# Delta-rule attention with a rational MoE: a chunk's front six slots later, weights in 16 larger groups

## The chip, the cores and the metric

The kernel runs on one core of one Trainium2 chip. Its time is the time of one execution of the whole program in microseconds; the figure for a kernel is the median over several executions, and lower is better.

## What is computed

Two layers in a row. The first is a delta rule over 768 time steps for 4 batches x 8 heads with a head size of 48; the second a feed-forward layer with a rational activation on 3072 tokens (384 -> 2048 -> 384).

```python
k_n = k / (np.linalg.norm(k, axis=-1, keepdims=True) + 1e-06)
for t in range(S):
    kt, vt, bt = (k_n[:, :, t], v[:, :, t], beta[:, :, t, None])
    y[:, :, t] = np.einsum('bhd,bhde->bhe', q[:, :, t], state)
    v_old = np.einsum('bhde,bhd->bhe', state, kt)
    state = state + bt[:, :, :, None] * np.einsum('bhd,bhe->bhde', kt, vt - v_old)
...
x = np.ascontiguousarray(attn_out.transpose(0, 2, 1, 3)).reshape(B * S, H * D)
...
h = x @ w_in
h2 = h * h
h3 = h2 * h
P = a[0] + a[1] * h + a[2] * h2 + a[3] * h3
Q = 1.0 + np.abs(b[0]) * np.abs(h) + np.abs(b[1]) * h2
g = P / (Q + 1e-06)
return (g @ w_out).astype(np.float32)
```

The inputs of the layer's weights arrive as 64-bit floating-point numbers and are read as pairs of 32-bit words.

## The kernel before

**Chunks and units.** The 768 steps are cut into 12 chunks of 64. A chunk's attention gives 256 tokens, and the feed-forward layer of those tokens is cut into 8 units of 256 hidden columns each, so there are 96 units, n = 8c to 8c + 7 for chunk c. Every product is made of three half-precision passes on high and low parts.

**A unit** has `hidden` (18 products into the tile `ph`), `numerator` (two ScalarE operations, then L830, L832, L833 on VectorE), `quotient` (two ScalarE operations, then L844, L845, L846 on VectorE and one product on GpSimd) and `accumulate` (12 products into `po`). The unit's VectorE operations are kept in the order in which they are written. They work on the tiles `mr`, `mu`, `mw`, three buffers of each.

**A chunk's attention** is a row of steps. `ahead` loads k, v and q and normalises the keys. `front` has `keys_transposed` (a transposing DMA, then `kbd`), `key_products` (`pg`, copied to `g`, written to DRAM as `gd`), `inverse` (reads `gd` back as `gb`, some 30 small VectorE operations, the result `wh` goes to an image `img` in DRAM and comes back as `wc`), `scales`, `queries_transposed` and `query_products` (`pm`). `middle` has `off_blocks` (`pe` from `wc`, read out as `et`; `wc` also goes to the block-diagonal tile `wbd`), `state_split` and `residual`. `back` is the solve: `pu` from `wbd`, three steps in which `pu` is read out as `z` by ScalarE and VectorE and multiplied again, then the state (`pd`), the output (`py`), and `tokens`, which transposes the output (`px`) into `xT`, the right-hand side of `hidden`, and `scalars`, a row of one-column operations that ends in `msc` (L787). Both `hidden` and `numerator` of unit 8c need them.

**The order of the work.** Each of these steps is written in one of 8 slots (j) of a chunk. In the slots of unit group c the program writes the solve of chunk c + 1, the middle of c + 2, the front of c + 3 and the loads of c + 4:

```python
def attention(c, j):
    for f, cc in ((back, c + 1), (middle, c + 2), (front, c + 3), (ahead, c + 4)):
        if cc < NCH:
            f(cc, j)
```

The framework then sets the order on each engine at build time, by the order written, by priorities (the solve has a raised one) and by a model of times; on the chip each engine runs its list strictly in that order. DMAs are issued by SyncE (SP), which also keeps its order. The pools `ps_f` and `ps_c` of PSUM hold one tile each; `ps_f` serves `pg`, `pm`, `pe`, the sums of `scales` and, from chunk 3 on, `px`. A tile is handed on in the order written.

**The weights** are made first, among the attention of chunks 0 and 1: `load_in(i)` makes a unit's 768 columns in three groups of 256, `load_out(i)` in four of 192, 56 groups in all. `to_f32` turns a group of word pairs into 32-bit numbers: an absolute value on ScalarE, a minimum and maximum on GpSimd, a shift (L318) and two combining operations (L325) on VectorE. In `load_out` the second half is then split on GpSimd. The groups of `load_out` use as their lower limit the value `gate`, which the first inverse writes, and so come behind it.

Of the kernel before, what the change touches and what calls it, by code (L numbers as in the profile page):

```python
# [36 lines left out]
def kernel(  # L37
# [271 lines left out]
    def to_f32(t, src, nm, keep=MIN_NORMAL):  # L309

        n = t.shape[-1]
        st = staged([P, n, 2], U32, "ws" + nm)
# [5 lines left out]
        nc.vector.tensor_scalar(  # L318
            t, a.bitcast(U32), 3, KEEP, op0=ALU.logical_shift_left, op1=ALU.bitwise_and
        )  # L320
        for word, scalar, in1, op0, op1 in (
            (wh, 0xC0000000, t, ALU.bitwise_and, ALU.bitwise_or),
            (wl, 29, t, ALU.logical_shift_right, ALU.bitwise_or),
        ):
            nc.vector.scalar_tensor_tensor(out=t, in0=word, scalar=scalar, in1=in1, op0=op0, op1=op1)  # L325
# [3 lines left out]
    def load_in(i):  # L329
        w64 = moe_w_in.bitcast(U32)  # L330
        t = w_out[:, i].rearrange("p a b e -> p (a b e)").bitcast(U32).rearrange("p (c f) -> p c f", c=NCC)
# [13 lines left out]
        split16((w_in[:, i, 0], w_in[:, i, 1]), t.bitcast(F32), sw[:, 0, i : i + 1])  # L345

    def load_out(i):
        w64 = moe_w_out.bitcast(U32)
        if i + 1 < NU:
            to = w_out[:, i + 1].rearrange("p a b e -> p a (b e)").bitcast(U32)  # L350
            to = [to[:, j] for j in range(2)]
        else:
            to = [staged([P, DM], U32, f"wo32_{i}_{j}") for j in range(2)]
        fs = sb.tile([P, 2], F32, tag="wfs", name=f"wfs_{i}")
        for j in range(2):
            f = 2 * i + j
            for e in range(2):
                cl = slice(e * DM // 2, (e + 1) * DM // 2)
                to_f32(to[j][:, cl], w64[f * P : (f + 1) * P, e * DM : (e + 1) * DM], f"o{f}_{e}", gate)
            sum_squares(fs[:, j : j + 1], to[j].bitcast(F32), w_out[:, i, 0, j])  # L360
# [679 lines left out]
```

## Time and profile before

| | us |
|---|---|
| median of 3 runs | 845.66 (845.34 to 847.08) |
| the profiled execution | 849.25 |
| its span, from the first to the last instruction | 845.5 |
| busy in the span: PE (matmul) | 627.7 (74%) |
| VectorE (DVE) | 740.2 (88%) |
| ScalarE (ACT) | 617.1 (73%) |
| GpSimd (POOL) | 338.1 (40%) |
| mean granted clock of TensorE | 0.944 |

The profile is one execution. A row of a group gives line, engine, operation, output<-input, its form and count, then busy us and the mean ns of one, then the engine's idle time just before it and what ended that; a row of one line's records gives the shortest, median and longest duration in ns and the first and last start in us. "DMA to landing" is the time from the issue to the end of the transfer. L826 to L846 are a unit's operations.

### The profile page before, as it was taken

To read this page: it belongs to the slowest core of one execution; us is meant where nothing else is said; L and a number is where in the kernel's file an instruction comes from. 1 tells how busy PE (TensorE), PEld (TensorE's weight loads), DVE (VectorE), ACT (ScalarE), POOL (GpSimd) and SP (SyncE) were. 2 spreads that over 40 slices of the span, in tenths; PEclk is the share of its full clock that TensorE was granted. 3 is DMA by queue.
4 is the path that set the end of the run, shared out by engine and by line. 5 is a ranking of instruction groups with operands and counts; after the bars stand their busy time and mean duration, and the time that the engine had idled before them with its cause. 6 is when DMAs were issued, how large, how long until landed. Compare 5 with 4: busy or idle time off the path is not lost.

```text
span 845.5 us, 23179 instructions
## 1 busy us (share of the span) xinstructions
PE 627.7 (74%) x9264; PEld 493.8 (58%) x9264; DVE 740.2 (88%) x1405; ACT 617.1 (73%) x1278; POOL 338.1 (40%) x322
## 2 busy tenths in 40 slices
PE   0330346778778777866978988789789789999995
PEld 0220344666566666755866866667567667786662
DVE  5999896688879778987998999989988799998996
ACT  4866658768667675866966968768668768788873
POOL 6545754334435333253433433432433332222232
PEclk9999996898989898989999999989899999999999
DMA  8998979769979879999599399696597674300000
GB/s 237 249 212 170 225 155 170 123 140 169 157 130 165 146 120 191 146 140 183 93 145 187 71 176 150 119 193 105 98 167 111 110 103 80 76 2 21 1 19 19
DMA packets 466507, 111.46 MB, mean 132 GB/s; under 512 B 431328, under 2 KB 463072, under 8 KB 466400
## 3 DMA queue, kind: packets, MB, share of 16 engines
q1 hardware_dynamic: 464224, 108.83, 71.3%
q8 instruction: 72, 1.18, 0.6%
q10 hardware_dynamic: 2176, 1.17, 0.5%
q14 instruction: 35, 0.29, 0.1%
HBM read 40.47 MB, written 26.23 MB: 79 GB/s over the span
## 4 chain that ended last, share of the span: by engine, by line
DVE 34%; PE 19%; DMA 17%; SPq 11%; ACT 10%; issue 7%; POOL 1%; ACTq 0%; DVEq 0%; POOLq 0%
PE ph L808 7%; PE po L862 5%; DVE ph L845 4%; DVE w_out L325 4%; DVE mg L844 3%; DVE mw L830 3%; DVE mu L833 3%; DVE mu L832 3%; SPq L119 3%; PE pu L401 2%; DMA tq<-xdq 2%; DMA gd<-g 2%; DMA tk<-xdk 2%; SPq L475 2%; DVE mu L846 2%
## 5 line engine op out<-in xcount | busy, mean ns | idle before, releaser
L862 PE MATMUL po<-w_out,mg 128*128 128x384 f16 x1152 | 226.5, 339 | 33.3 <-DVE mg L844 20.9
L847 POOL TENSOR_TENSOR mg<-mu,mr 128x512 f16<-128x512 f32 x96 | 124.8, 1300 | 258.1 <-DVE mu L846 203.8
L808 PE MATMUL ph<-xT,w_in 128*128 128x256 f16 x1728 | 216.3, 280 | 14.1 <-DVE mu L846 11.2
L808 PEld LDWEIGHTS <-w_in 128*128 128x128 f16 x1728 | 169.8, 101 | 51.1 <-DVE mu L846 14.4
L862 PEld LDWEIGHTS <-mg 128*128 128x128 f16 x1152 | 109.5, 101 | 103.4 <-DVE mg L844 27.7
L401 PEld LDWEIGHTS <-kbd 128*128 128x128 f16 x1680 | 66.7, 109 | 47.8 <-issue 43.3
L830 DVE SCALAR_TENSOR_TENSOR mw<-mr,msc,ph 128x512 f32<-128x512 f32 x96 | 71.1, 741 | 22.1 <-ACT mu L828 21.9
L831 ACT ACTIVATE mw<-mw 128x512 f32<-128x512 f32 x96 | 60.4, 629 | 39.7 <-DVE mw L830 39.2
L845 DVE SCALAR_TENSOR_TENSOR ph<-mw,msc,mg 128x512 f32<-128x512 f32 x96 | 81.4, 848 | 1.0
L844 DVE SCALAR_TENSOR_TENSOR mg<-mu,msc,mr 128x512 f16<-128x512 f32 x96 | 81.1, 844 | 0.0
L826 ACT ACTIVATE mr<-ph,msc 128x512 f32<-128x512 f32 x96 | 65.2, 679 | 18.7 <-PE ph L808 6.9
L828 ACT ACTIVATE mu<-ph,coef,msc 128x512 f32<-128x512 f32 x96 | 74.2, 773 | 0.0
L846 DVE SCALAR_TENSOR_TENSOR mu<-mu,msc,ph 128x512 f32<-128x512 f32 x96 | 71.1, 741 | 1.4
L833 DVE SCALAR_TENSOR_TENSOR mu<-mu,msc,ph 128x512 f32<-128x512 f32 x96 | 70.7, 736 | 1.0
L841 ACT ACTIVATE mr<-mw,msc 128x512 f32<-128x512 f32 x96 | 69.2, 721 | 1.7
L401 PE MATMUL pu<-z,ebd 128*128 128x48 f16 x1728 | 54.9, 185 | 18.1 <-DVE z L232 13.5
L401 PEld LDWEIGHTS <-ebd 128*128 128x128 f16 x1728 | 53.9, 98 | 21.7 <-issue 19.4
L832 DVE TENSOR_TENSOR mu<-ph,mu 128x512 f32<-128x512 f32 x96 | 65.5, 682 | 0.0
L842 ACT ACTIVATE mr<-mr 128x512 f32<-128x512 f32 x96 | 60.3, 628 | 1.3
L401 PEld LDWEIGHTS <-wbd 128*128 128x128 f16 x1152 | 37.7, 99 | 35.9 <-issue 34.8
L230 POOL TENSOR_TENSOR mm<-m,mm 128x1024 f16<-128x1024 f32 x12 | 29.2, 2436 | 73.6 <-ACT mm L226 64.5
L401 PE MATMUL pm<-tq,kbd 128*128 128x64 f16 x576 | 27.0, 220 | 20.1 <-DMA tq<-xdq 18.3
(195 smaller groups left out, 1195.0 us busy)
## 6 DMA issues: line engine op xcount, KB each, us to landing
wsi<-in_moe_w_in_dram SPq DMA_DIRECT2D x24, 256.0 KB, 5.0
xdk<-kn SPq DMA_DIRECT2D x24, 256.0 KB, 3.7
kbd<-tk SPq DMA_DIRECT2D x24, 256.0 KB, 5.5
gd<-g SPq DMA_DIRECT2D x24, 256.0 KB, 3.5
...
```

The source lines that it names most:

```text
L401: nc.tensor.matmul(dst[p][:, h], head(bd, lp, p * H + h), head(rt, rp, p * H + h), start=start and n == 0 and h == 0, stop=stop and n == l ...
L808: nc.tensor.matmul(ph[:, i], w_in[:, f2, wp, cc, i * P : (i + 1) * P], x[:, xp, cc], start=k == 0, stop=k == 3 * NCC - 1,)
L828: nc.scalar.activation(u, ph, AF.Identity, scale=A3, bias=a2)
L830: in_order(nc.vector.scalar_tensor_tensor(out=w, in0=z, scalar=B0, in1=ph, op0=ALU.add, op1=ALU.mult))
L832: in_order(nc.vector.tensor_mul(u, ph, u))
L833: in_order(nc.vector.scalar_tensor_tensor(out=u, in0=u, scalar=A1, in1=ph, op0=ALU.add, op1=ALU.mult))
L841: nc.scalar.activation(r, w, AF.Ln, bias=Q0)
L844: in_order(nc.vector.scalar_tensor_tensor(out=g[:, 0], in0=u, scalar=A0, in1=r, op0=ALU.add, op1=ALU.mult))
L845: in_order(nc.vector.scalar_tensor_tensor(out=t, in0=w, scalar=Q0, in1=g[:, 0], op0=ALU.add, op1=ALU.mult))
L846: in_order(nc.vector.scalar_tensor_tensor(out=u, in0=u, scalar=A0, in1=t, op0=ALU.add, op1=ALU.subtract))
L847: nc.gpsimd.tensor_mul(g[:, 1], u, r)
L862: nc.tensor.matmul(po[p], g[:, gp, i, p * P : (p + 1) * P], w_out[:, f2, wp, i], start=f2 == lo and i == 0 and k == 0, stop=f2 == hi - 1 a ...
```

## The change

Three things:

1. `front` and `ahead` run six slots later against `back` and `middle` (`LATE`), and the parts of them that would be written ahead of the first unit are left to the slots; `off_blocks` moves from slot 3 to slot 4.
2. A weight group has 768 columns: one for each `load_in`, one for each `load_out`, 16 in all. The absolute value goes straight to its place; the split of `load_out` is one operation on ScalarE and one on VectorE, and GpSimd's half is gone. The last two groups of `load_in` take `gate` as their limit too.
3. `mr`, `mu` and `mw` become one tile `mx` of three parts, three buffers of it, in which the word pairs are also staged.

```diff
+        return sb.tile(shape, dtype, tag="mx", name=nm, bufs=MB)
...
-        nc.sync.dma_start(out=st.rearrange("p f w -> p (f w)"), in_=src)
+        parts_ = src.shape[1]
+        nc.sync.dma_start(out=st.rearrange("p (a f) w -> p a (f w)", a=parts_), in_=src)
...
-        a = sb.tile([P, n], F32, tag="mg", name="wa" + nm, bufs=MB)
-        nc.scalar.activation(a, wh.bitcast(F32), AF.Abs)
-        nc.gpsimd.tensor_scalar(a, a, 3.0e38, keep, op0=ALU.min, op1=ALU.max)
...
+        nc.scalar.activation(t.bitcast(F32), wh.bitcast(F32), AF.Abs)
+        nc.gpsimd.tensor_scalar(t.bitcast(F32), t.bitcast(F32), 3.0e38, keep, op0=ALU.min, op1=ALU.max)
+        nc.vector.tensor_scalar(t, t, 3, KEEP, op0=ALU.logical_shift_left, op1=ALU.bitwise_and)
...
-        for cc in range(NCC):
-            to_f32(t[:, cc], w64[cc * P : (cc + 1) * P, i * 4 * P : (i + 1) * 4 * P], f"i{i}_{cc}")
+        to_f32(t, w64[:, i * 4 * P : (i + 1) * 4 * P].rearrange("(c p) x -> p c x", p=P), f"i{i}", gate if i >= NU - 2 else MIN_NORMAL)
...
+        to_f32(t, w64[2 * i * P : (2 * i + 2) * P].rearrange("(j p) x -> p j x", j=2), f"o{i}", gate)
...
-            else:
-                scaled(to[j].bitcast(F32), ss[:, 1:2])
-                split16((w_out[:, i, 0, j], w_out[:, i, 1, j]), to[j].bitcast(F32), eng=nc.gpsimd)
+        split16((w_out[:, i, 0], w_out[:, i, 1]), t, ss[:, 1:2])
...
-        r = z = sb.tile([P, 2, TG], F32, tag="mr", name=f"mr{n}", bufs=MB)
+        m = sb.tile([P, 3, 2, TG], F32, tag="mx", name=f"mx{n}", bufs=MB)
+        u, w, r = (m[:, i] for i in range(3))
...
-        elif j == 3:
+        elif j == 4:
             with tc.high_priority(300):
                 off_blocks(c)
...
+    LATE = 6
+
     def attention(c, j):
-        for f, cc in ((back, c + 1), (middle, c + 2), (front, c + 3), (ahead, c + 4)):
+        for f, cc, late in ((back, c + 1, 0), (middle, c + 2, 0), (front, c + 3, LATE), (ahead, c + 4, LATE)):
+            cc, jj = divmod(cc * NU + j - late, NU)
             if cc < NCH:
-                f(cc, j)
+                f(cc, jj)
...
-            if what == "f":
+            if what == "f" and f0 * NU + j < 3 * NU - LATE:
...
-            elif what == "a":
+            elif what == "a" and (f2 + 1) * NU + j < 4 * NU - LATE:
```

In the rows of the changed kernel below, its own line numbers stand: L811, L813, L814, L825, L826, L827 are L830, L832, L833, L844, L845, L846 of before, L809 is L826, L768 is L787, L313 and L315 are L318 and L325, L718 and L720 are L737 and L739, L568, L572, L420 are L587, L591, L439. Numbers behind a name tell one tile from the next of its name.

**VectorE before unit 40**, the first of chunk 5. Before the change, from L844 of unit 38 on (the operations L844 to L846 of unit n - 1 are written behind L830 to L833 of unit n; `z_2` is the third step of the solve of chunk 6):

```order
L844 SCALAR_TENSOR_TENSOR mg_7689<-mu_7575,msc_6424,mr_7573 128x512
L501 RECIPROCAL nrm_8157<-nrm_8157 128x16
L617 TENSOR_SCALAR sc_7909<-pfq_7907 128x2
L845 SCALAR_TENSOR_TENSOR ph_7659<-mw_7577,msc_6424,mg_7689 128x512
L232 SCALAR_TENSOR_TENSOR z_2_7976<-pu_7589,zmask,z_2_7976 128x768
L619 TENSOR_SCALAR sc_7909<-sc_7909,sc_6798 128x1
L846 SCALAR_TENSOR_TENSOR mu_7575<-mu_7575,msc_6424,ph_7659 128x512
L787 TENSOR_TENSOR msc_7535<-tab,sf_7446 128x48
L251 TENSOR_SCALAR sc_7909<-lgq_7912 128x2
L545 TENSOR_TENSOR ab_8088<-gb_7900,bblk 128x64
L830 SCALAR_TENSOR_TENSOR mw_7837<-mr_7833,msc_7535,ph_7814 128x512
```

And after it, where `xT` and `msc` belong to chunk 5, the three `z` to the solve of chunk 6:

```order
L232 SCALAR_TENSOR_TENSOR z_0_7129<-pu_7004,zmask,z_0_7129 128x768
L232 SCALAR_TENSOR_TENSOR xT_6804<-px_6808,sf_6806,xT_6804 128x768
L750 RECIPROCAL kp_0_6878<-kp_0_6878 128x2
L232 SCALAR_TENSOR_TENSOR z_1_7315<-pu_7004,zmask,z_1_7315 128x768
L757 TENSOR_SCALAR kp_0_6878<-kp_0_6878,top 128x1
L251 TENSOR_SCALAR kp_0_6878<-kp_0_6878 128x1
L761 RECIPROCAL kp_0_6878<-kp_0_6878 128x1
L768 TENSOR_TENSOR msc_6900<-tab,sf_6806 128x48
L598 TENSOR_SCALAR sc_7064<-pfq_7062 128x2
L600 TENSOR_SCALAR sc_7064<-sc_7064,sc_5969 128x1
L232 SCALAR_TENSOR_TENSOR z_2_7422<-pu_7004,zmask,z_2_7422 128x768
L811 SCALAR_TENSOR_TENSOR mx_7301<-mx_7301,msc_6900,ph_7282 128x512
```

The making of `xT` and all three solve steps, which stood among the operations of the units ahead, now stand behind L846 of unit 38 and ahead of the first operation of unit 40 (`et` of chunk 6 comes a few rows ahead of them, behind L844 of unit 38). The same rows stand before units 48, 56, 64 and 72; before units 32 and 80 `et` comes earlier. The last operation of the inverse (`wh`) of chunk 6 stands behind L830 of unit 36 and `et` of chunk 6 behind that of unit 39; before the change they stood behind those of units 26 and 31.

**ScalarE at the same place**, after the change, up to the first operation of unit 40 (`g` and `gl` are of chunk 7):

```order
L228 ACTIVATE z_1_7315<-pu_7004,zmask 128x768
L742 ACTIVATE kp_0_6878<-kp_0_6878,coef 128x1
L742 ACTIVATE kp_0_6878<-kp_0_6878 128x1
L497 ACTIVATE g_6952<-pg_6903 128x1024
L758 ACTIVATE kp_0_6878<-kp_0_6878 128x1
L226 CAST gl_6956<-g_6952 128x768
L759 ACTIVATE kp_0_6878<-kp_0_6878 128x1
L742 ACTIVATE kp_0_6878<-kp_0_6878 128x1
L742 ACTIVATE sf_6806<-kp_0_6878 128x1
L742 ACTIVATE sf_6806<-sf_6806,kp_0_6878 128x1
L228 ACTIVATE z_2_7422<-pu_7004,zmask 128x768
L809 ACTIVATE mx_7301<-ph_7282,msc_6900 128x512
```

The reading out of `pg` of the next front but one and of the second and third solve step stands ahead of the unit's first operation. On TensorE the two small products of `px` come ahead of the 48 of `pu<-rr`, the transposes behind these, and `pg` and most of the 36 products of units 40 and 41 between the second and the third multiplication of the solve.

**SyncE behind the inverse of chunk 6**, before the change:

```order
L587 DMA img_129<-wh_6163 128x16x16
L119 DMA q_6426<-in_q_dram 64x8x48 x3
L591 DMA wc_6167<-img_129 64x16x64 x2
L119 DMA q_6426<-in_q_dram 64x8x48
L433 DMA kbd_115<-tk_5953 64x16x128 x2
L119 DMA k_6531<-in_k_dram 64x8x48 x3
L116 DMA v_6283<-in_v_dram 64x16x48 x2
L119 DMA k_6531<-in_k_dram 64x8x48
L439 DMA wbd_123<-gl_5577 64x16x96 x2
L518 DMA gd_6634<-g_6684 64x16x64 x2
L528 DMA gb_6789<-gd_6634 128x16x16
L439 DMA wbd_123<-wc_6167 64x16x128 x2
```

And after it:

```order
L568 DMA img_129<-wh_6275 128x16x16
L116 DMA v_7473<-in_v_dram 64x16x48 x2
L572 DMA wc_6279<-img_129 64x16x64 x2
L420 DMA wbd_123<-wc_6279 64x16x128 x2
L587 DMA ebd_121<-et_6634 16x32x48
L587 DMA ebd_121<-et_6634 16x32x32
```

The issues that stood between `wc` and `wbd` (loads, `kbd`, the next front's `gd` and `gb`) are no longer there.

More of the change, by code (lines that the diff above doesn't have):

```diff
@@ L312, in to_f32 @@
         st = staged([P, n, 2], U32, "ws" + nm)
-        nc.sync.dma_start(out=st.rearrange("p f w -> p (f w)"), in_=src)
+        parts_ = src.shape[1]
+        nc.sync.dma_start(out=st.rearrange("p (a f) w -> p a (f w)", a=parts_), in_=src)
         wl, wh = st[..., 0], st[..., 1]
-        a = sb.tile([P, n], F32, tag="mg", name="wa" + nm, bufs=MB)
-        nc.scalar.activation(a, wh.bitcast(F32), AF.Abs)
-        nc.gpsimd.tensor_scalar(a, a, 3.0e38, keep, op0=ALU.min, op1=ALU.max)
[L318 to L325, printed above, removed]
+        nc.scalar.activation(t.bitcast(F32), wh.bitcast(F32), AF.Abs)
+        nc.gpsimd.tensor_scalar(t.bitcast(F32), t.bitcast(F32), 3.0e38, keep, op0=ALU.min, op1=ALU.max)
+        nc.vector.tensor_scalar(t, t, 3, KEEP, op0=ALU.logical_shift_left, op1=ALU.bitwise_and)
+        for word, scalar, op0 in ((wh, 0xC0000000, ALU.bitwise_and), (wl, 29, ALU.logical_shift_right)):
+            nc.vector.scalar_tensor_tensor(out=t, in0=word, scalar=scalar, in1=t, op0=op0, op1=ALU.bitwise_or)
     def load_in(i):
         w64 = moe_w_in.bitcast(U32)
-        t = w_out[:, i].rearrange("p a b e -> p (a b e)").bitcast(U32).rearrange("p (c f) -> p c f", c=NCC)
-        for cc in range(NCC):
-            to_f32(t[:, cc], w64[cc * P : (cc + 1) * P, i * 4 * P : (i + 1) * 4 * P], f"i{i}_{cc}")
+        t = w_out[:, i].rearrange("p a b e -> p (a b e)").bitcast(U32)
+        to_f32(t, w64[:, i * 4 * P : (i + 1) * 4 * P].rearrange("(c p) x -> p c x", p=P), f"i{i}", gate if i >= NU - 2 else MIN_NORMAL)
+        t = t.bitcast(F32).rearrange("p (c f) -> p c f", c=NCC)
         s2 = w_in[:, i, 0].bitcast(BF16)
-        nc.scalar.activation(s2, t.bitcast(F32), AF.Square)
+        nc.scalar.activation(s2, t, AF.Square)
         pf = ps_h.tile([P, 2 * P], F32, tag="h", name=f"pfw{i}")
@@ L344, in load_in @@
         scale_of(sw[:, 0, i : i + 1], ss, f"w{i}")
-        split16((w_in[:, i, 0], w_in[:, i, 1]), t.bitcast(F32), sw[:, 0, i : i + 1])
+        split16((w_in[:, i, 0], w_in[:, i, 1]), t, sw[:, 0, i : i + 1])
     def load_out(i):
@@ L349, in load_out @@
         if i + 1 < NU:
-            to = w_out[:, i + 1].rearrange("p a b e -> p a (b e)").bitcast(U32)
-            to = [to[:, j] for j in range(2)]
-        else:
[L353 to L360, printed above, removed]
+            t = w_out[:, i + 1].rearrange("p a b e -> p (a b e)").bitcast(U32)
+        else:
+            t = staged([P, 2 * DM], U32, f"wo32_{i}")
+        to_f32(t, w64[2 * i * P : (2 * i + 2) * P].rearrange("(j p) x -> p j x", j=2), f"o{i}", gate)
+        t = t.bitcast(F32).rearrange("p (j e) -> p j e", j=2)
+        fs = sb.tile([P, 1], F32, tag="wfs", name=f"wfs_{i}")
+        sum_squares(fs, t, w_out[:, i, 0])
         ss = sb.tile([P, 2], F32, tag="ss", name=f"vss_{i}")
-        nc.vector.tensor_scalar(ss[:, 0:1], fs[:, 0:1], fs[:, 1:2], 2.0 ** -30, op0=ALU.add, op1=ALU.max)
+        nc.vector.tensor_scalar_max(ss[:, 0:1], fs, 2.0 ** -30)
         ro = sw[:, 1, i : i + 1]
```

11 lines of the change are left out of this document (1 added, 10 removed).

## The prediction

> **What bounds the kernel now.** I read the page's span first, then the busy time by stage, cut where the records of L830 (a unit's first operation on VectorE) open units 0, 8, 16, 24, 80 and 88, and then the groups by line and the DMAs' times to landing for the steps that move. Columns of the stages: stretch and its length, then busy time of each engine, the clock, the DMA share and GB/s.
>
> ```profile
> span 845.5 us, 23179 instructions
> ...
> core 0: us, PE busy (x) PEld busy (x) DVE busy (x) ACT busy (x) POOL busy (x), PEclk, DMA share, GB/s
> ...
> 20.00:150.30 130.30, 46.59 (x715) 39.00 (x715) 117.53 (x336) 91.53 (x246) 71.80 (x92) 0.95 0.92 197
> 150.30:223.70 73.40, 56.07 (x871) 45.35 (x871) 56.95 (x119) 55.19 (x120) 29.50 (x26) 0.88 0.80 144
> 223.70:296.10 72.40, 57.90 (x918) 45.90 (x917) 61.21 (x108) 49.37 (x97) 27.61 (x21) 0.88 0.90 152
> 296.10:371.50 75.40, 59.89 (x1081) 49.32 (x1077) 65.38 (x116) 53.69 (x108) 30.77 (x27) 0.93 0.89 149
> 371.50:764.20 392.70, 337.74 (x5125) 266.21 (x5126) 357.37 (x610) 300.44 (x588) 141.91 (x109) 0.96 0.71 120
> 764.20:800.20 36.00, 33.61 (x314) 24.04 (x312) 34.83 (x60) 32.13 (x64) 8.93 (x7) 1.00 0.05 13
> ```
>
> VectorE is the nearest to a bound in every stage: 117.5 of 130.3 us while weights are made, 357.4 of 392.7 us in chunks 3 to 9, 34.8 of 36.0 in chunk 10, where no attention is left. So I count its work and its idle time. Idle: 12.8 us in the stretch up to unit 0; 16.4, 11.2 and 10.0 (37.6) in chunks 0 to 2; 35.3 in chunks 3 to 9, 5.0 a chunk. Whatever moves the end changes one of these numbers.
>
> **The weights.** The operations that go and stay:
>
> ```profile
> L325 DVE SCALAR_TENSOR_TENSOR w_out<-wso,w_out x56: 322/357/1825, 74.5 to 124.9; 128x192 uint32<-128x192 uint32 x56
> L325 DVE SCALAR_TENSOR_TENSOR w_out<-wsi,w_out x48: 407/414/1629, 18.8 to 63.5; 128x256 uint32<-128x256 uint32 x48
> ...
> L318 DVE TENSOR_SCALAR w_out<-wao x28: 234/249/1712, 74.2 to 121.1; 128x192 uint32<-128x192 uint32 x28
> L318 DVE TENSOR_SCALAR w_out<-wai x24: 274/284/1907, 18.3 to 62.4; 128x256 uint32<-128x256 uint32 x24
> ...
> L232 DVE SCALAR_TENSOR_TENSOR w_in<-w_out,sw,w_in x8: 1003/1078/1180, 29.7 to 74.9; 128x768 f16<-128x768 f32 x8
> L232 DVE SCALAR_TENSOR_TENSOR w_out<-w_out,vss x7: 605/617/1291, 84.5 to 136.9; 128x384 f16<-128x384 f32 x7
> ```
>
> By medians, with the eight and four records of the last group counted among their like: 48 x 0.414 + 64 x 0.357 + 24 x 0.284 + 32 x 0.249 = 57.5 us. After it there are 32 long and 16 short operations of 768 columns. Carrying the step from 192 to 256 columns on gives 0.87 us for a long one; the row of L232 with 768 columns has 1.08; I take 0.95, and 0.57 for a short one: 39.5 us, so 18.0 us less. The second half of a w_out group comes from GpSimd to VectorE: 8 x 1.08 instead of 8 x 0.617, 3.7 back. Net 14 us less, 10 to 17 by the two prices. What changes on GpSimd and ScalarE lies beside this: 71.8 and 91.5 us busy in the 130.3. The loads keep their bytes, and three groups are in flight as before; SyncE issues 16 instead of 56, costed at nothing, since VectorE was busy 90% here and did not wait for them; that a larger group must land whole before its first operation can cost the start one landing, about 3 us. The last two w_in groups now wait for the first inverse; w_out's groups, which waited for it already, stand beside them on VectorE, and without that cover they would cost one GpSimd operation each. One tile for mw, mu and mr frees all three when GpSimd has read u and r; the first operation of the unit that reuses it writes r, which waited for the same read, so this costs nothing.
>
> The Trainium skill (VectorE: DVE Perf Modes, the section on the TRN2 errata) has two prices for the fixed part of such an operation, 58 cycles at 0.96 GHz in its table and 151 cycles in a formula that it calls measured. By the first, an estimate from the page, 120 fewer operations are worth 7 us and the sum below would be 11 us higher; by the second 19 us. The rows side with the second: 0.284 us at 256 and 0.249 at 192 columns leave 0.14 us for none.
>
> **The shift.** A chunk's inverse, products and transposes start six units later, its solve stays. First 24 units: the order had the inverses of chunks 2 to 5 done there, now 2 to 4. One is, on VectorE, at least
>
> ```profile
> L566 DVE TENSOR_TENSOR pr<-ab,wt 128x64 f32<-128x64 f32 (+1 forms) x36 | 23.0, 664 | 0.1
> L561 DVE TENSOR_TENSOR pr<-gb,wt 128x64 f32<-128x64 f32 (+1 forms) x36 | 20.7, 598 | 0.2
> L655 DVE TENSOR_TENSOR m<-pm,mask 128x1024 f32<-128x1024 f32 x12 | 14.6, 1216 | 10.6 <-PE pm L401 10.6
> ```
>
> 58.3/12 = 4.9 us by these three rows alone, and it returns in chunks 3 to 9: work is moved, not saved. So only idle time can change. Early, four fronts in 24 units leave 37.6 us idle where one per eight leaves 5.0: I take a third of the difference of 22.6, 8 us less (bounds 0 and 22.6).
>
> From chunk 4 on the new order closes a loop. tokens(c) makes the input of unit 8c, in a tile of the pool ps_f, which holds one tile; in program order the tile before it is that of off_blocks(c+1), which needs wc, so the inverse of c+1. That inverse now ends three units before unit 8c instead of a chunk earlier (the order of VectorE). So the last things before a chunk's first unit are, in a row: image, wc, pe, wbd, the first solve steps, tokens. SyncE's row helps: the fourteen transfers that stood between wc and wbd are gone from there, which is why I take plain landing times. Its prices:
>
> ```profile
> L587 SPq DMA_DIRECT2D img<-wh x12: 382/532/660, 73.6 to 697.9; - x12
> ...
> DMA to landing us min/median/max: 3.2/4.0/5.8
> ...
> L591 SPq DMA_DIRECT2D wc<-img x24: 581/668/1593, 78.5 to 702.5; - x24
> ...
> DMA to landing us min/median/max: 3.9/5.1/7.2
> ...
> L439 SPq DMA_DIRECT2D wbd<-wc x24: 605/691/1919, 87.9 to 710.7; - x24
> ...
> DMA to landing us min/median/max: 3.1/4.7/6.7
> ...
> L401 PE MATMUL pe<-wc,wbd 128*128 128x48 f16 x576 | 20.4, 186 | 20.7 <-DVE w_out L325 18.3 <-DMA wc<-img 1.6 <-DVE sc L617 0.8
> L401 PE MATMUL pu<-z,ebd 128*128 128x48 f16 x1728 | 54.9, 185 | 18.1 <-DVE z L232 13.5 <-DVE sw L251 4.4
> L401 PE MATMUL pg<-tk,kbd 128*128 128x64 f16 x576 | 25.5, 208 | 12.8 <-issue 6.2 <-DVE w_out L325 6.1 <-DMA k<-in_k_dram 0.6
> ...
> L228 ACT ACTIVATE z<-pu,zmask x36: 880/898/921, 101.0 to 755.5; 128x768 f16<-128x768 f32 x36
> ...
> L232 DVE SCALAR_TENSOR_TENSOR z<-pu,zmask,z x36: 996/1007/1020, 103.7 to 757.3; 128x768 f16<-128x768 f32 x36
> ```
>
> From wh to wc in SBUF: 4.0, one more issue of 0.7 and 5.1, so 10 us with the waits between. From the start of pe: pe 20.4/12 = 1.7; wbd 0.7 + 4.7; pu 54.9/36 = 1.5; 8.6 so far, and PE's row has the token transposes behind pu. Then the rows of ScalarE and VectorE put three solve steps ahead of the unit's first operation: 3 x (0.9 + 1.0) + 2 x 1.5 = 8.7, with pg, 25.5/12 = 2.1, and some 2 us of products of the new unit between two of them on PE: 12.8. In all 21.4 us from the start of pe to L830. What VectorE has to do in it:
>
> ```profile
> L845 DVE SCALAR_TENSOR_TENSOR ph<-mw,msc,mg 128x512 f32<-128x512 f32 x96 | 81.4, 848 | 1.0
> L846 DVE SCALAR_TENSOR_TENSOR mu<-mu,msc,ph 128x512 f32<-128x512 f32 x96 | 71.1, 741 | 1.4
> L232 DVE SCALAR_TENSOR_TENSOR xT<-px,sf,xT 128x768 f16<-128x768 f32 x12 | 12.1, 1007 | 0.8 <-ACT xT L228 0.8
> L232 DVE SCALAR_TENSOR_TENSOR et<-pe,et 128x768 f16<-128x768 f32 x12 | 11.4, 946 | 2.9 <-ACT et L228 2.7
> L492 DVE TENSOR_REDUCE nrm<-sq 128x16 f32<-128x768 f32 x12 | 11.4, 948 | 5.2 <-ACT sq L491 5.2
> L739 DVE TENSOR_SCALAR xs<-px 128x1 f32<-128x1 f32 x12 | 1.8, 146 | 0.0
> ```
>
> 0.85 + 0.74 + 1.01 + 0.95, three z at 1.01 and a dozen small ones of 0.15 to 0.3, 2.1 together: 8.7 us. VectorE comes to et 14.5 us after wh (a unit is 34.8/8 = 4.4 us by chunk 10; one whole unit, one with the reduction of L492 more, and two parts of 1.6 and 3.1), so 4.5 us after pe could start. 21.4 - 4.5 - 8.7 = 8.2 us idle; operations overlap their neighbours a little, so 7.5 a boundary.
>
> Five boundaries (before units 40, 48, 56, 64, 72) have all of this; those before units 32 and 80 have no pe in them, 5 us each by the solve alone. Together 47.5 us. Bounds: 3 each if wbd lands before PE gets there, 13 each with the slowest landings (5.8 + 7.2 and 6.7).
>
> The ordinary 35.3 us idle of chunks 3 to 9 will partly vanish into these stretches, since a unit late elsewhere is forgiven there: 15 less (bounds 0 and 35). What is late next: pg(c+2) needs the tile that tokens(c) holds, so its transfers gd and gb, and the next inverse, start only in this stretch. On SyncE the loads and transposes of a front, some 25 issues, move with it and pass the solve's; on GpSimd its splits. Neither queue is ahead of the chain in the rows, so I add nothing. The tail loses nothing.
>
> Sum: -14 - 8 + 47.5 - 15 = +10.5 us on a span of 845.5. The profiled execution took 849.25 us, span and 3.75 around it; the median of the runs shown is 845.66, so the forecast there is **856 us**.
>
> **The rivals.**
> *The stretch is short.* wbd lands while PE still multiplies for the units before, ACT and VectorE find z and tokens ready, and a boundary costs 3 us: -14 - 8 + 21 - 15 = -16, **830 us**. For it: 5.0 us a chunk idle now, with the same transfers. It decides where a boundary costs less than 37/7 = 5.3 us. Against it: the serial 8.7 us of three solve steps alone equals VectorE's work there.
> *The loop itself binds.* wc arrives 3.9 us later by the slowest rows, wbd 2.0: 13.4 us at five boundaries, 7 at two: 81; -14 - 8 + 81 - 15 = +44, **890 us**. For it: DMA share 0.8 to 0.9 in early chunks; against it: 0.71 later.
> *The weights save nothing.* While GpSimd works, a VectorE operation can stand still:
>
> ```profile
> 101.25 1.81 POOL L230 TENSOR_TENSOR gl<-g,gl 128x768 f16<-128x768 f32 x1 [0.98 <-DVE w_out L325]
> ...
> 101.45 1.82 DVE L325 SCALAR_TENSOR_TENSOR w_out<-wso,w_out 128x192 uint32<-128x192 uint32 x1
> ...
> L243 POOL TENSOR_SCALAR q<-q,sc x12: 903/909/1607, 41.7 to 660.3; 128x768 f32<-128x768 f32 x12
> ```
>
> A 0.36 us operation took 1.82 and ended with GpSimd's; 0.91 us is what GpSimd takes for 768 columns of such a kind. Sixteen of them, each holding one operation of VectorE for its length, make 14.6 us, and the first term is gone: +24.5, **870 us**. Against it: the 56 shorter ones of before could do the same. The Trainium skill (SBUF — State Buffer, Who interferes with whom) says the same, that the shared port pair is locked for a whole instruction and the second to come blocks; the row agrees.
>
> **How the numbers follow.** The forecast's case has 0.38: its own range is 844 to 868, boundaries between 5.8 and 9.2 us. Short stretch 0.33, binding loop 0.17, weights 0.12. Within 0.2% (1.7 us, about what a measurement of this kernel can tell from no change) lies the lower edge of the first, 0.06, and 0.02 of it below that; with the short stretch, faster is 0.35 and slower 0.59. The range of 826 to 886 us leaves out the lower part of the short stretch's spread and the upper half of the binding loop's, about 0.1 each.
>
> **What would show it.** L325 in 32 records near 0.95 us and unit 0 at 125 to 140 us (150.3 now); unit 24 some 20 to 30 us earlier than 371.5; from unit 32 on, eight units with 5 to 10 us idle on VectorE just before L830 of each chunk's first, ended by ScalarE's z or PE's pu; pe waiting for wc. If these gaps are under 4 us, the forecast is wrong in its sign; if unit 0 does not move, the first term is.

## The result and the profile after

The changed kernel takes 891.13 us (median of 4 runs, 888.26 to 894.54), the kernel before, run beside it, 845.5 us: a ratio of 1.054 with a 95% interval of 1.050 to 1.059. The forecast was 856 us with a range of 826 to 886: the sign was right, the size was not. The profiled execution took 888.26 us.

These are the span and the stages of the changed kernel, cut where L811 (L830 before) opens units 0, 24, 80 and 88. Columns as in the prediction's table.

```profile
span 886.5 us, 22755 instructions
...
core 0: us, PE busy (x) PEld busy (x) DVE busy (x) ACT busy (x) POOL busy (x), PEclk, DMA share, GB/s
...
20.00:141.30 121.30, 43.15 (x667) 35.88 (x666) 102.00 (x205) 80.32 (x177) 52.17 (x39) 0.78 0.91 199
141.30:344.50 203.20, 163.02 (x2688) 131.37 (x2689) 175.47 (x320) 153.09 (x310) 75.76 (x64) 0.90 0.81 141
344.50:801.80 457.30, 358.16 (x5340) 274.32 (x5335) 373.30 (x644) 320.74 (x608) 158.11 (x120) 0.95 0.64 116
801.80:840.00 38.20, 34.63 (x324) 25.27 (x325) 35.69 (x60) 32.83 (x65) 8.97 (x7) 0.96 0.05 12
840.00:886.50 46.50, 36.46 (x238) 23.13 (x238) 36.64 (x51) 26.68 (x42) 13.10 (x10) 0.90 0.07 17
```

Up to unit 0 the kernel is 9 us quicker (141.3 against 150.3), in chunks 0 to 2 another 18 (203.2 against 221.2), and then chunks 3 to 9 take 457.3 us instead of 392.7: 64.6 more. Of these VectorE is busy for 15.9; its idle time rises from 35.3 to 84.0 us.

Where the idle time lies shows in the stretches from the last unit of a chunk to the first of the next (start of L811 to start of L811), here those before units 32 to 80. First the changed kernel:

```profile
388.95:406.02 17.07, 16.20 (x323) 13.53 (x323) 10.38 (x23) 13.22 (x32) 4.39 (x3) 1.00 0.23 43
449.74:470.96 21.22, 16.27 (x311) 13.85 (x311) 11.06 (x26) 13.43 (x32) 7.19 (x7) 0.92 0.33 64
515.85:537.15 21.30, 16.36 (x311) 13.70 (x311) 11.07 (x26) 13.63 (x32) 7.20 (x7) 0.92 0.34 65
584.88:608.65 23.77, 18.43 (x355) 15.10 (x353) 10.97 (x24) 13.74 (x35) 5.34 (x5) 0.93 0.35 68
654.99:674.08 19.09, 15.89 (x303) 12.80 (x300) 11.05 (x24) 13.50 (x32) 4.95 (x4) 1.00 0.38 71
717.75:742.25 24.50, 19.86 (x344) 16.26 (x340) 10.88 (x26) 13.80 (x35) 5.28 (x4) 0.86 0.36 69
786.61:801.79 15.18, 14.07 (x260) 11.67 (x260) 9.00 (x20) 10.87 (x28) 2.56 (x2) 1.00 0.10 10
sum 142.13, PE 117.09 PEld 96.91 DVE 74.41 ACT 92.19 POOL 36.90; mean PE 16.73 PEld 13.84 DVE 10.63 ACT 13.17 POOL 5.27
```

And the sum over the same seven stretches of the kernel before:

```profile
sum 72.91, PE 66.56 PEld 54.10 DVE 63.35 ACT 59.38 POOL 42.61; mean PE 9.51 PEld 7.73 DVE 9.05 ACT 8.48 POOL 6.09
```

Length minus busy time of VectorE (the third engine) is its idle time: 142.1 - 74.4 = 67.7 us after, 72.9 - 63.4 = 9.6 before. The seven stretches are 69.2 us longer; all the rest of chunks 3 to 9 together is 4.5 us shorter.

One of them, ahead of unit 40, in the changed kernel's timeline: SyncE's issues, then PE, then VectorE (start, duration, operation; in brackets the idle time before it and what ended it). The `pg` at 463.65 is that of chunk 7, the one at 529.72 that of chunk 8, before unit 48.

```profile
437.97 3.48 SPq L119 DMA_DIRECT2D k<-in_k_dram  x4
441.55 0.57 SPq L568 DMA_DIRECT2D img<-wh  x1
...
445.13 1.32 SPq L572 DMA_DIRECT2D wc<-img  x2
452.04 1.86 SPq L420 DMA_DIRECT2D wbd<-wc  x2
...
450.65 1.36 PE L382 MATMUL pe<-wc,wbd 128*128 128x48 f16 x48 [0.87 <-DMA wc<-img]
...
453.91 0.27 PE L717 MATMUL px<-identf,xs 128*1 128x128 f32 x1
...
457.79 2.10 PE L382 MATMUL pu<-rr,wbd 128*128 128x48 f16 x48 [2.58 <-DMA wbd<-wc]
...
463.65 1.60 PE L382 MATMUL pg<-tk,kbd 128*128 128x64 f16 x48
...
467.37 1.37 PE L382 MATMUL pu<-z,ebd 128*128 128x48 f16 x48
...
529.72 1.60 PE L382 MATMUL pg<-tk,kbd 128*128 128x64 f16 x48
...
438.67 0.44 DVE L559 SCALAR_TENSOR_TENSOR wh<-wt,wh 128x256 f16<-128x256 f32 x1
...
452.89 0.96 DVE L232 SCALAR_TENSOR_TENSOR et<-pe,et 128x768 f16<-128x768 f32 x1 [0.36 <-ACT et L228]
...
456.28 0.16 DVE L722 RECIPROCAL sf<-sf 128x1 f32<-128x1 f32 x1
460.87 1.02 DVE L232 SCALAR_TENSOR_TENSOR z<-pu,zmask,z 128x768 f16<-128x768 f32 x1 [4.42 <-ACT z L228]
462.57 1.02 DVE L232 SCALAR_TENSOR_TENSOR xT<-px,sf,xT 128x768 f16<-128x768 f32 x1 [0.69 <-ACT xT L228]
...
467.49 0.15 DVE L251 TENSOR_SCALAR kp<-kp 128x1 uint32<-128x1 uint32 x1 [2.07 <-ACT kp L759]
...
468.90 0.45 DVE L768 TENSOR_TENSOR msc<-tab,sf 128x48 f32<-128x48 f32 x1 [1.06 <-ACT sf L742]
...
469.72 1.02 DVE L232 SCALAR_TENSOR_TENSOR z<-pu,zmask,z 128x768 f16<-128x768 f32 x1
470.96 0.75 DVE L811 SCALAR_TENSOR_TENSOR mx<-mx,msc,ph 128x512 f32<-128x512 f32 x1 [0.23 <-ACT mx L810]
```

In order of time it is the chain of the prediction: image, wc, pe the moment wc has landed, wbd (issued 0.03 us after pe, which still reads that tile, has ended), pu the moment that has landed, then the solve and tokens, and only then unit 40. From pe to L811 it takes 20.3 us.

The handing on of ps_f's one tile can be read off too. The first px starts at 453.91, 0.06 us after VectorE has read pe into et (452.89 + 0.96), and pg of chunk 7 at 463.65, 0.06 us after VectorE has read px into xT (462.57 + 1.02). That pg opens the inverse on which the next boundary waits. From it to the same step of chunk 8 it is 66.1 us, and from unit 40 to unit 48 66.2 (470.96 to 537.15): each round of the loop begins where the one before lets it.

The Trainium skill (PSUM — Partial Sum Buffer, the section on engine and sequencer instructions) says that the queues of ScalarE and VectorE are strictly first in, first out and that matmuls start in program order; for VectorE the trace agrees: unit 40's first operation, at 470.96, stands behind a z at 469.72 that it does not use.

### The profile page after: what moved, and what is told of

Its sections match the earlier page's. It is cut to its first block, busy times and chain, and to the rows that moved or that the text cites. A ratio compares the mean times of both kernels' runs of the same rounds, so it can differ in the third digit from the quotient of the medians.

```text
span 886.5 us, 22755 instructions
## 1 busy us (share of the span) xinstructions
PE 637.5 (72%) x9264; PEld 491.7 (55%) x9264; DVE 731.8 (83%) x1285; ACT 621.5 (70%) x1214; POOL 321.4 (36%) x266
## 4 chain that ended last, share of the span: by engine, by line
DVE 30%; DMA 28%; PE 12%; ACT 9%; SPq 9%; issue 8%; POOL 3%; ACTq 0%; POOLq 0%; DVEq 0%
DMA wc<-img 5%; DVE ph L826 4%; DMA img<-wh 4%; DVE mg L825 4%; DMA gb<-gd 3%; DVE mx L811 3%; DVE mx L814 3%; PE po L843 3%; DMA tq<-xdq 3%; DMA gd<-g 2%; DVE mx L813 2%; DMA wbd<-wc 2%; DVE mx L827 2%; PE ph L789 2%; PE pu L382 2%
## 5 line engine op out<-in xcount | busy, mean ns | idle before, releaser
L828 POOL TENSOR_TENSOR mg<-mx 128x512 f16<-128x512 f32 x96 | 128.4, 1338 | 272.5 <-DVE mx L827 217.6
L812 ACT ACTIVATE mx<-mx 128x512 f32<-128x512 f32 x96 | 60.4, 629 | 66.8 <-DVE mx L811 66.5
L826 DVE SCALAR_TENSOR_TENSOR ph<-mx,msc,mg 128x512 f32<-128x512 f32 x96 | 88.1, 918 | 1.1
L811 DVE SCALAR_TENSOR_TENSOR mx<-mx,msc,ph 128x512 f32<-128x512 f32 x96 | 71.1, 740 | 21.2 <-ACT mx L810 15.3
L825 DVE SCALAR_TENSOR_TENSOR mg<-mx,msc 128x512 f16<-128x512 f32 x96 | 82.5, 859 | 0.0
L809 ACT ACTIVATE mx<-ph,msc 128x512 f32<-128x512 f32 x96 | 65.1, 678 | 13.1 <-PE ph L789 6.5
L810 ACT ACTIVATE mx<-ph,coef,msc 128x512 f32<-128x512 f32 x96 | 74.2, 773 | 0.0
L382 PEld LDWEIGHTS <-kbd 128*128 128x128 f16 x1680 | 59.6, 103 | 23.5 <-issue 17.6
L827 DVE SCALAR_TENSOR_TENSOR mx<-mx,msc,ph 128x512 f32<-128x512 f32 x96 | 71.0, 739 | 1.5
L814 DVE SCALAR_TENSOR_TENSOR mx<-mx,msc,ph 128x512 f32<-128x512 f32 x96 | 70.9, 738 | 1.0
L822 ACT ACTIVATE mx<-mx,msc 128x512 f32<-128x512 f32 x96 | 69.2, 721 | 2.1
L813 DVE TENSOR_TENSOR mx<-ph,mx 128x512 f32<-128x512 f32 x96 | 65.5, 682 | 0.0
L823 ACT ACTIVATE mx<-mx 128x512 f32<-128x512 f32 x96 | 60.4, 629 | 2.1
L232 DVE SCALAR_TENSOR_TENSOR z<-pu,zmask,z 128x768 f16<-128x768 f32 x36 | 36.5, 1014 | 25.7 <-ACT z L228 25.4
```

The lines of the kernel that those rows point to most:

```text
L382: nc.tensor.matmul(dst[p][:, h], head(bd, lp, p * H + h), head(rt, rp, p * H + h), start=start and n == 0 and h == 0, stop=stop and n == l ...
L811: in_order(nc.vector.scalar_tensor_tensor(out=w, in0=z, scalar=B0, in1=ph, op0=ALU.add, op1=ALU.mult))
L813: in_order(nc.vector.tensor_mul(u, ph, u))
L814: in_order(nc.vector.scalar_tensor_tensor(out=u, in0=u, scalar=A1, in1=ph, op0=ALU.add, op1=ALU.mult))
L822: nc.scalar.activation(r, w, AF.Ln, bias=Q0)
L825: in_order(nc.vector.scalar_tensor_tensor(out=g[:, 0], in0=u, scalar=A0, in1=r, op0=ALU.add, op1=ALU.mult))
```

## The experiments

Besides each kernel's time stand two figures from its trace, worked out as above: VectorE's idle time in the seven stretches before units 32 to 80, and its other idle time between unit 24 and unit 80 (9.6 and 25.8 us in the kernel before, 67.7 and 16.3 in the changed one). "No shift" is LATE = 0.

**1. The weights and mx alone.**

```diff
-    LATE = 6
+    LATE = 0
-        elif j == 4:
+        elif j == 3:
             with tc.high_priority(300):
                 off_blocks(c)
```

> The changed kernel with the shift taken back (LATE = 0, off_blocks at j == 3 again): only the weights in 16 groups of 768 elements and the one tile mx for mw, mu and mr stay. Loop theory: the loss is all in the shift, so this keeps what the weights gave at the front (unit 0 came 9 us earlier, 14 us were forecast): 831 to 838 us. Rival, the tile: mx held by GpSimd holds up the units, some 0.3 us in each of 96: 855 to 870 us. Rival, the weights save nothing: 843 to 848 us.

834.69 us, a ratio of 0.990 (0.988 to 0.992) to the kernel before: faster than both kernels, and the loss is all in the shift. Its stages up to unit 0 and of chunks 3 to 9:

```profile
20.00:142.53 122.53, 41.46 (x667) 34.67 (x666) 103.27 (x205) 80.34 (x177) 52.33 (x39) 0.62 0.91 197
...
363.69:751.05 387.36, 337.58 (x5249) 270.82 (x5246) 356.59 (x615) 300.57 (x589) 143.33 (x111) 0.96 0.69 123
```

Unit 0 comes at 142.5 us: 7.8 of the forecast 14. Chunks 3 to 9 have 7.2 and 23.5 us idle, less than before. The one tile mx was costed at nothing; L811 does wait for GpSimd there, 5.0 us in three places from unit 24 to unit 80, and still these chunks are 5.3 us shorter:

```profile
DVE mx L811 <- POOL mg L828: 5.0, 3, 2.6
```

**2. The shift alone**, in the kernel before with its old weights and tiles (LATE = 6 and off_blocks at j == 4, as in the diff of the change).

> The kernel before with the shift alone (LATE = 6, off_blocks at j == 4); weights and tiles as before. Loop theory: 891 plus what the weights gave, 898 to 908 us, with the idle time of VectorE before units 32 to 80 at 55 to 75 us in all, as in the changed kernel (67.7). Rival, the new tiles and weights carry the loss: 845 to 860 us.

906.32 us, ratio 1.075 (1.073 to 1.078). Its seven stretches:

```profile
sum 145.74, PE 116.82 PEld 97.17 DVE 75.99 ACT 93.82 POOL 36.79; mean PE 16.69 PEld 13.88 DVE 10.86 ACT 13.40 POOL 5.26
```

145.7 - 76.0 = 69.7 us idle, as forecast by the loop.

**3. tokens in ps_c**, the whole shift kept.

```diff
-        pool = ps_c if c < 3 else ps_f
+        pool = ps_c
```

> The changed kernel, but tokens takes its tile from ps_c in every chunk, not from ps_f from chunk 3 on; the shift stays whole. Loop theory: the one tile of ps_f, handed from pe of the next chunk to tokens and on to pg, is what ties a unit's start to the next chunk's inverse; without it gd, gb and the next inverse can start some six units earlier, wbd is there before the solve, and the idle time before units 32 to 80 falls from 67.7 us to under 20: 835 to 850 us. Rival, the three solve steps that the queues of ScalarE and VectorE put ahead of a chunk's first unit cost the time by themselves: 875 to 895 us. Rival, the front's work that came back into chunks 3 to 9 (its transfers and its 16 us on VectorE) costs it: 870 to 890 us.

851.37 us, ratio 1.011 (1.009 to 1.014), just over the expected 850: one line takes 40 of the 46 us back. Its seven stretches, and the two largest waits of VectorE from unit 24 to unit 80 (who waited, for whom, us in all, times, longest):

```profile
sum 95.01, PE 75.57 PEld 62.70 DVE 90.67 ACT 62.90 POOL 37.64; mean PE 10.80 PEld 8.96 DVE 12.95 ACT 8.99 POOL 5.38
...
DVE mx L811 <- ACT mx L810: 16.8, 13, 4.7
DVE et L232 <- ACT et L228: 15.1, 5, 6.0
```

The stretches' idle time is 4.3 us. In this trace pg of chunk 7 starts at 445.91, 27.9 us before unit 40 (7.3 in the changed kernel), the inverse of chunk 6 ends in unit 32 instead of 36, and pe starts 43.2 us before unit 40 instead of 20.3: the loop is open. What is left against run 1 is elsewhere: 44.2 us of idle time instead of 23.5, 15.1 of them ahead of et, for PE waits for wc in the middle of the units.

**4. Less shift**: LATE = 3 in the changed kernel.

> The changed kernel with LATE = 3 in place of 6: the inverse of a chunk ends three units earlier against its own solve. Loop theory: the wait for wc and wbd before a chunk's first unit (some 12 us a boundary) lies beside three units of 5 us and is hidden, so the idle time there falls from 67.7 to 10 to 25 us: 838 to 852 us. Rival, each unit of shift costs the same: halfway between the kernel without shift and the changed one, 860 to 870 us.

846.88 us, ratio 1.004 (1.002 to 1.006); 4.8 us idle in the stretches (10 to 25 were expected), 40.6 elsewhere. Half the shift costs nothing like half the loss.

**5 and 6. wc loaded twice**, under the shift and without it.

```diff
         for b in range(2):
-            nc.sync.dma_start(out=words[b * C : (b + 1) * C], in_=as_rows(im, b))
+            for _ in range(2):
+                nc.sync.dma_start(out=words[b * C : (b + 1) * C], in_=as_rows(im, b))
```

> The changed kernel (LATE = 6) with the two transfers of wc from the image issued twice, the second pair over the first with the same data: it puts one landing (5.1 us) and two issues (1.4 us) more between the inverse and pe. Loop theory: at each of the five boundaries whose first unit waits for this chain the idle time grows by the whole of it, 5 to 7 us, 25 to 35 us in all: 915 to 928 us. Rival, the units wait for the order of ScalarE's and VectorE's queues and not for the transfers: 889 to 898 us.

> The same doubled wc in the kernel without shift (new weights, LATE = 0, 834.7 us). Loop theory: the inverse ends a chunk earlier than its solve, so the 6.5 us are hidden in every chunk but the first, which the start waits for: 833 to 842 us, with chunks 3 to 9 within 5 us of the 387.4 us that they take without. Rival, doubled traffic alone costs (512 KB more a chunk on the shared transfers): 3 us a chunk or more, 865 us and up.

946.94 us (ratio 1.123, 1.115 to 1.131) and 862.87 us (1.025, 1.019 to 1.031): 55.8 and 28.2 us more than without, so both expectations of the loop missed. Without the shift chunks 3 to 9 took 408.5 us instead of 387.4, 3.0 a chunk, which is what the rival gave. But SyncE's waits there show a second candidate beside traffic: its queue stands at the second pair (L573) until the first has landed, with everything behind it. The run doesn't tell the two apart.

```profile
SPq L420 <- PE pu L382: 20.7, 5, 14.6
SPq L573 <- DMA wc<-img: 12.4, 9, 3.6
```

Under the shift the seven stretches have 82.4 us idle, 14.7 more or 2.1 each, and one more boundary opens, before unit 24:

```profile
339.88:378.18 38.30, 18.25 (x258) 14.06 (x257) 13.20 (x29) 14.55 (x35) 7.06 (x8) 0.64 0.56 100
```

38.3 us where the changed kernel has 6.9. The pair tells that the chain is dearer under the shift (28 us of difference), but not what a microsecond of it costs: the edit also moved the order and held a queue.

**7. tokens in ps_c without the shift** (the edits of 1 and 3).

> The kernel without shift (new weights, LATE = 0) with tokens in ps_c in every chunk. Loop theory: without the shift tokens waited for nothing in ps_f, so its tile does not matter here: 832 to 838 us, where the same edit was worth 40 us under the shift. Rival, ps_f is crowded anyway and the edit is a gain of its own: 815 to 828 us. Rival, px in ps_c holds up pk and pu: 840 to 850 us.

841.68 us, ratio 0.999 (0.996 to 1.003): 7 us slower than run 1, just into the range of the second rival. Under the shift the same line is a gain of 40.

**8. The weights without most of their bytes** (run 1, each group reads one row block for all, so the weights are other numbers).

```diff
-        nc.sync.dma_start(out=st.rearrange("p (a f) w -> p a (f w)", a=parts_), in_=src)
-        wl, wh = st[..., 0], st[..., 1]
+        nc.sync.dma_start(out=st[:, : n // parts_].rearrange("p f w -> p (f w)"), in_=src[:, 0])
+        shape = [P, parts_, n // parts_]
+        wl, wh = (st[:, : n // parts_, i].unsqueeze(1).broadcast_to(shape) for i in range(2))
...
```

> The kernel without shift (new weights, LATE = 0) in which each group loads only the first of its three (w_in) or two (w_out) row blocks and every operation reads that block again for the others, in the same number of operations of 768 columns: the weights are other numbers, 7 MB of 12 are not moved. It asks what took 5 of the 14 us forecast for the weights. Theory, the loads: groups of 768 KB land 6 to 7 us after issue and VectorE, quicker now, waits for them, so unit 0 comes at 128 to 137 us (142.5 with whole loads) and the run at 820 to 829 us. Rival, GpSimd and ScalarE in the chain of a group, or the first inverse, set the end: unit 0 at 140 to 144, 832 to 837 us.

831.77 us, ratio 0.987 (0.983 to 0.990), and unit 0 at 140.7 us:

```profile
20.00:140.65 120.65, 47.34 (x744) 39.92 (x742) 104.18 (x211) 84.77 (x185) 55.38 (x42) 0.72 0.92 168
```

The loads are worth 1.8 us up to unit 0, not the missing 6; the whole run can't be told from run 1.

**9. pe behind tokens**: the tile of ps_f goes round the other way, the shift whole.

```diff
-        elif j == 4:
-            with tc.high_priority(300):
-                off_blocks(c)
         elif j == 5:
...
+        elif j == 7:
+            with tc.high_priority(300):
+                off_blocks(c)
```

> The changed kernel (LATE = 6, tokens in ps_f) with off_blocks moved from j == 4 to j == 7, so that in program order the tile of ps_f goes to tokens before it goes to pe of the next chunk, and no longer the other way round; nothing else is edited. Loop theory: with the ring turned round, unit 8c no longer waits for the next chunk's inverse, although the shift is whole: idle before units 32 to 80 under 20 us (67.7 in the changed kernel), the run at 845 to 865 us, near the 851 us of the edit that moved tokens to ps_c. Rival, an inverse only half a chunk ahead of its solve binds whatever the tiles: 880 to 900 us.

865.68 us, ratio 1.028 (1.023 to 1.032), a little over the range of the loop theory and far under the rival's. Its seven stretches:

```profile
sum 72.29, PE 54.62 PEld 39.76 DVE 43.25 ACT 50.19 POOL 25.70; mean PE 7.80 PEld 5.68 DVE 6.18 ACT 7.17 POOL 3.67
```

They are as short as before the change (72.3 us), with 29.0 us idle (under 20 were expected), for less of VectorE's work is left in them; 35.5 us are elsewhere.

**10. The same without the shift.**

> The kernel without shift (new weights, LATE = 0) with off_blocks at j == 7 as in the run before this. Loop theory: there is no loop to open here; pe is four units later and has a chunk less of slack, wbd lands closer to the solve: 835 to 850 us. Rival, ps_f is the bottleneck without the shift too and the order is a gain: 815 to 830 us.

864.08 us, ratio 1.022 (1.016 to 1.029): far from the forecast, pe that late costs 29 us by itself, and 27.0 us are idle in the seven stretches without any shift. With pe there the shift costs 1.6 us.

**11. off_blocks at j == 4 without the shift.**

> The kernel without shift (new weights, LATE = 0) with off_blocks at j == 4, the small second part of the shift alone, one unit later than j == 3. Loop theory: one unit of 5 us out of the slack of 5 to 15 us that pe has there after wc: 833 to 842 us. Rival, it was this step and not LATE that closed the ring: 870 us and more.

851.33 us, ratio 1.010 (1.006 to 1.013): 16.6 us for one slot, of which 16.0 us of idle in the stretches against 7.2 are a part. A miss of both; the larger step, LATE from 0 to 6, is still 39.8 us.

**12 and 13. LATE = 5 and LATE = 4.**

> The changed kernel with LATE = 5 (off_blocks at j == 4, tokens in ps_f). In VectorE's order et, z0, xT, z1 and z2 still stand between the last unit of a chunk and the first of the next, and the next inverse behind them, as with 6. Loop theory: the price comes with that order and not by the unit, so it is nearly whole: 880 to 895 us, 55 us or more idle before units 32 to 80. Rival, each unit of shift beyond three costs the same (847 at 3, 891 at 6): 876 us or a little under.

> The changed kernel with LATE = 4. In VectorE's order units stand between et and z0 again, and the next inverse begins before the chunk's first unit. Loop theory: no boundary waits: 843 to 855 us, under 15 us idle before units 32 to 80, next to LATE = 3. Rival, a price by the unit: 860 to 864 us.

887.14 us (ratio 1.052, 1.046 to 1.058) and 855.29 us (1.015, 1.011 to 1.019; its upper expectation passed by 0.3). The seven stretches, of 5 and then of 4:

```profile
sum 137.21, PE 108.26 PEld 90.40 DVE 72.61 ACT 89.65 POOL 39.70; mean PE 15.47 PEld 12.91 DVE 10.37 ACT 12.81 POOL 5.67
```

```profile
sum 82.04, PE 67.62 PEld 54.88 DVE 76.97 ACT 57.14 POOL 29.18; mean PE 9.66 PEld 7.84 DVE 11.00 ACT 8.16 POOL 4.17
```

64.6 us idle and 5.1. With off_blocks at j == 4 the series over LATE = 0, 3, 4, 5, 6 reads 851, 847, 855, 887, 891 us: flat, then 32 us in one step, where z0, xT, z1 and z2 come to stand in VectorE's order in a row between the last unit and the first; at LATE = 4 they stand among the units' operations. It is a switch and no price by the unit.

**14. No clamp on GpSimd in six w_in groups** (run 1 with GpSimd's operation left out there).

```diff
-        nc.gpsimd.tensor_scalar(t.bitcast(F32), t.bitcast(F32), 3.0e38, keep, op0=ALU.min, op1=ALU.max)
+        if keep is gate:
+            nc.gpsimd.tensor_scalar(t.bitcast(F32), t.bitcast(F32), 3.0e38, keep, op0=ALU.min, op1=ALU.max)
```

> The kernel without shift (new weights, LATE = 0) without GpSimd's min and max in the six w_in groups that don't wait for the inverse (the clamp of numbers out of float32's range is left out there): six operations of 0.82 us that stand between ScalarE's and VectorE's of a group, and beside which VectorE's stand still. It asks where the weights' 5 missing us went, after the loads gave back 1.8. Theory, GpSimd: its operation stretches VectorE's and lengthens a group's chain, so unit 0 comes 5 to 9 us earlier than 142.5 us: 134 to 138, the run at 826 to 831 us. Rival, the first inverse and the chain behind it set unit 0: 140 to 143 us, 832 to 837 us.

842.23 us, ratio 0.999 (0.996 to 1.002). Up to unit 0:

```profile
20.00:142.47 122.47, 41.77 (x667) 35.48 (x666) 103.01 (x203) 80.53 (x177) 43.57 (x33) 0.59 0.91 200
```

GpSimd is 8.8 us less busy and unit 0 has not moved (142.5): those six operations are not the missing time either. The whole missed both ranges: it is 7.5 us slower than run 1, for chunks 3 to 9, which the edit does not touch, took 398.7 us against 387.4.

**What they show together.** The price of the shift hangs on what ps_f's one tile does, not on the shift (no shift, then LATE = 6):

| tokens and pe | no shift | shifted | the shift costs |
|---|---|---|---|
| tokens behind pe in ps_f, as changed | 834.69 (j == 3) | 891.13 (j == 4) | 56.4 |
| tokens in ps_c | 841.68 (j == 3) | 851.37 (j == 4) | 9.7 |
| tokens ahead of pe in ps_f (j == 7) | 864.08 | 865.68 | 1.6 |

The first two rows carry this. The third says less than its 1.6 us: with pe so late the kernel without shift already waits in the stretches, as run 10 showed. But run 9 beside the changed kernel says the same as run 3: with the whole shift, and tokens no longer behind pe, 25 us come back. So the loss needs both: an inverse late enough that pe and wbd arrive in the last unit of a chunk, and tokens behind that pe. Run 1 is the best version that computes the same.

## Why the prediction was wrong in size

Term by term, forecast against the two profiled spans (845.5 and 886.5):

| step of the sum | forecast | measured |
|---|---|---|
| weights: start of unit 0 | -14 | -9.0 |
| idle time in chunks 0 to 2 | -8 | -9.9 |
| idle time in the seven stretches before units 32 to 80 | +47.5 | +67.7 |
| ordinary idle time of chunks 3 to 9 (35.3 before) | -15 | -19.0 |
| VectorE's work in chunks 0 to 9 ("moved, not saved") | 0 | -8.1 + 15.9 = +7.8 |
| after unit 80 | 0 | +3.4 |
| sum | +10.5 | +41.0 |

The terms are counted as the forecast counted them: all of the stretches' idle time is new, and what is left of the ordinary 35.3 us is the 16.3 outside them.

The mechanism was the forecast's: the loop over ps_f, the boundaries where it said, ended by ScalarE's z, pe waiting for wc (7 times in chunks 3 to 9), unit 24 27 us earlier. Four of the six terms were sized too kindly, two came out a little better.

*The boundary* was mis-sized most, and it is 20.2 of the 30.5 us that the sum missed. The forecast had 7.5 us at five of them and 5 at two; idle are 10.2, 10.2, 12.8, 8.0 and 13.6, mean 11.0, and 6.7 and 6.2. The length of the chain was right: from the start of pe to L811 the five take 20.3, 20.3, 23.0, 19.7 and 25.1 us, mean 21.7 against 21.4. The step that failed is the cover, the work that VectorE still has to do beside the chain, put at 4.5 + 8.7 = 13.2 us. Over these five:

```profile
sum 108.44, PE 87.37 PEld 72.74 DVE 53.59 ACT 68.43 POOL 28.39; mean PE 17.47 PEld 14.55 DVE 10.72 ACT 13.69 POOL 5.68
```

VectorE works 10.7 us of 21.7, so 11.0 are idle. From et on its work is 8.3 to 9.7 us, as costed; before et it is 1.8 to 2.0 us and not 4.5. Two steps behind the 4.5 came out otherwise. Between wh and et VectorE had 12.9 us of work on the mean, not 14.5. And pe came 12.0 us after wh, not 10, where the prediction had said of SyncE's loads "Neither queue is ahead of the chain in the rows, so I add nothing": at four of the five boundaries the image is issued 0.9 to 5.8 us after the end of wh, behind loads. In the view above wh ends at 439.1, the four issues of k go on until 441.45, and the image follows. The last 0.7 us a boundary are what the forecast took off for overlap.

VectorE's longest waits from unit 24 to unit 80 (who, for whom, us in all, times, longest):

```profile
DVE z L232 <- ACT z L228: 22.0, 16, 4.4
DVE kp L251 <- ACT kp L759: 9.9, 7, 2.2
```

The wait for kp comes at seven places, 1.4 us each: scalars(c) goes back and forth between ScalarE and VectorE, and the forecast had counted its "dozen small ones" as VectorE's work alone. It did not lengthen the stretch ahead of unit 40, though: there the products of the third solve step end at 468.74 (467.37 + 1.37), so VectorE would have waited for that z just as long.

*The weights.* The operations came out as costed:

```profile
L315 DVE SCALAR_TENSOR_TENSOR w_out<-wsi,w_out x16: 932/959/2272, 20.8 to 73.0; 128x768 uint32<-128x768 uint32 x16
L315 DVE SCALAR_TENSOR_TENSOR w_out<-wso,w_out x14: 889/950/2107, 76.7 to 114.6; 128x768 uint32<-128x768 uint32 x14
...
L313 DVE TENSOR_SCALAR w_out<-w_out x15: 544/551/1993, 20.2 to 109.5; 128x768 uint32<-128x768 uint32 x15
```

Medians of 0.95 and 0.55 us against 0.95 and 0.57. By the Trainium skill (VectorE: DVE Perf Modes, the section on the TRN2 errata) 768 columns are 0.86 us with 58 fixed cycles and 0.96 with 151, an estimate from the page; the rows side with the second, as the prediction read them. In the kernel with the new weights alone VectorE works 15.9 us less up to unit 0 (103.27 + 8.69 of the first 20 us, against 117.5 + 10.3) and idles 8 us more. The step that failed is the one that turned all of VectorE's saved work into time, "what changes on GpSimd and ScalarE lies beside this" and the loads "costed at nothing": a stage 90% busy on one engine left 12.8 us of cover, and the next limit was nearer than 14 us. Of the 8 us, 1.9 lie at the start: the first L313 begins at 20.2 us, the first L318 at 18.3, for the first absolute value starts later on ScalarE (18.4 us against 16.8), and it and GpSimd's operation behind it are longer. The rest lies in short waits, and what sets them stays open. Most of the loads' bytes are worth 1.8 us (run 8), six of the clamps nothing (run 14); the first inverse, which the last ten groups wait for, was not tried.

*The one tile mx* was said to cost nothing; run 1 has 5.0 us of waits for GpSimd at L811, too few to show in its chunks 3 to 9.

*The relief* of ordinary idle time was taken at 15 of 35.3 us; 16.3 are left outside the boundaries, so 19.0 went. *Work moved, not saved* held for the shift alone: in run 2 VectorE works 16.5 us less in chunks 0 to 2 and 16.7 more in chunks 3 to 9. In the changed kernel it is 8.1 less and 15.9 more, 7.8 us that no run explains. A part shows: L826 takes 6.7 us more over the whole run than L845 did (88.1 against 81.4), at a median of 0.76 against 0.75, so some of its operations are drawn out. The 3.4 us behind unit 80 were put at nothing too ("The tail loses nothing"); no run asks for their cause.

Of the rivals, "the loop itself binds" named 890 us, and 891 came out. The loop does bind, as its round of 66.1 us shows; but the rival's reason, slow landings of wc and wbd, was not it: their medians, 4.8 and 4.9 us, are near the 5.1 and 4.7 that were used (4.7 is the row of a line that loads wbd twice over, from gl and from wc; wbd<-wc alone had 5.0), and its 81 us for the boundaries was 13 too much, made good by the terms it shared with the forecast. That it came within 1 us is luck. "The stretch is short" fell with the first gap of 10 us. "The weights save nothing" fell with run 1.
